# A planner's rule for split loads: a SyncE transfer no longer waits, in the virtual clock, for another part of its tile

## The chip, the cores and the metric
One core of one Trainium2 chip runs the program. The metric is the device time of one execution in microseconds (us). Three runs of the kernel before took 1041.17, 1041.32 and 1042.38 us; the median is 1041.32. A separate execution was profiled: it took 1042.86 us, and its span, from the first to the last instruction, is 1040.8 us.

## What is computed
Agent attention, then a mixture of experts in which each token goes to its best expert. B=4 batches, N=11456 tokens, C=128 channels, 49 agents, 8 experts, 1024 hidden columns, all float32.

```python
a2k = sm(agents, k)              # softmax of scaled products, 49 x N
agent_v = a2k @ v                # 49 x 128
q2a = sm(q, agents)              # N x 49
x = (q2a @ agent_v).reshape(B * N, 128)
e_idx = argmax(x @ w_gate)       # one expert for each token
for e in range(8):
    h = maximum(x[mask] @ w1[e], 0)
    out[mask] = gate_w * sigmoid(x @ w_output_gate)[e] * (h @ w2[e])
```

## The kernel before, in words
**Tiles and stages.** A batch is cut into 12 units, eleven of 1024 tokens and one of 192. For each unit of k the program makes scores `ks`, for each unit of v a share of the average `av`, and for each unit of q scores `qs`. The scores of q become weights `e16` (float16 pairs on 49+49+30 rows), which a transposing DMA turns into the tile `x1`. The last 19 rows of these pairs are then copied by four small DMAs, 19 partitions x 1024 columns of float16 (38 KB) each, into four places of a second tile `x2` (rows 32g to 32g+19, lines 1022 and 1023). A token's most frequent expert in the batch is picked first (`fold`, line 779): its weights `w1t`, `w2t` are loaded by an index read on SyncE (`ei`, line 834), folded with the average into `aw` and `w`, and the main stream runs all tokens through that expert. A tile of the main stream (512 tokens, 92 in all) has 16 matmuls `h` (for two halves, four from `x1`, four from `x2`) and 64 matmuls `y`. Between them ScalarE makes `hh` and VectorE makes `hl`, the high and low halves of the hidden layer. The few tokens of other experts are gathered and done again near the end (`let`, `lx`, `lh`, `ly`).

**What sets the order.** Every engine runs its own instructions in the order in which the program was written out, and that order comes from a planner. The planner keeps a virtual clock (`Clock`, from line 55): a time for each engine and one for the DMA engines together, and for each tile the time when it is written (`ready`) and read (`read`). Each piece of work is a coroutine that offers its next instruction; `can` (line 108) lets it through if the virtual clock says that its operands are there, and `issue` (line 120) or `emit` (line 195) books its cost. If nothing fits, TensorE's virtual time goes on by 40 ns, or, before the first tile of the main stream, a filler matmul `warm` is written out. So a wait in the virtual clock is no wait on the chip: it is other instructions, or fillers, put in front. On the chip an instruction waits for its own semaphores, whatever the plan thought.

**DMAs in the virtual clock.** A transfer from SyncE (SP) is booked in `emit`: it starts 1100 ns after SP issues it, or when the DMA engines are free, takes its bytes at 360 bytes per ns, and its tile is ready 950 ns later. For 19 x 1024 values this comes to 216 ns. The tile's `writer` is then "DMA":

```python
q = c.vt["DMA"] = max(c.vt["DMA"], t + 1100.0) + n * (2.46 if turned else 4.0) / 360.0
...
    c.ready[x.name] = max(c.ready.get(x.name, 0.0), q + (2500.0 if turned else 950.0))
    c.writer[x.name] = "DMA"
```

SP's own time goes on by 480 ns for each. In `at` (line 84) an instruction that writes a tile waits until the tile is ready, unless its own engine wrote it. For a second transfer into the same tile the engine is "SP" and the writer "DMA", so the rule holds it back until the transfer before has landed.

**Around the change.** Tiles that SP writes in parts: `x2` (four parts, 48 units), `w1t` (two halves, four batches), the first unit of k (two halves, line 592), and `wgo`. In `q_rest` (line 991) the order is: transposing DMA into `x1`, the four parts of `x2`, then the gate matmuls `lg` from `x1`; each `yield` must pass before the next is offered. The main stream takes a unit only when `x1` and `x2` are ready in the virtual clock (`can1` in `main_stream`, line 1245). Once the main stream has started, a matmul that reads a DMA's tile is held 1500 ns longer (`LANDS`, line 52); before that there is no margin. Loads go into 7 large places that become free when TensorE has read them, `x1` and `x2` into 8 small ones.

Of the kernel before, what the change touches and what calls it, by code (L numbers as in the profile page):

```python
# [15 lines left out]
SP = mybir.EngineType.SP  # L16
# [38 lines left out]
class Clock:  # L55
# [28 lines left out]
    def at(self, ins, outs=(), eng=None, late=None):  # L84

        t = 0.0
        for x in ins:
            if x.name not in self.apart:
                w = self.writer.get(x.name)
                if w == "DMA" and late is not None:  # L90
                    more = self.margin
                else:
                    more = 0.0 if w in (eng, "PE") else late or 0.0
                t = max(t, self.ready.get(x.name, 0.0) + more)
        for x in outs:
            n = x.name
            if n in self.apart:
                continue
            if self.writer.get(n) != eng:
                t = max(t, self.ready.get(n, 0.0))  # L100
            t = max(t, self.read.get(n, 0.0), self.free_at(n))
        return t
# [158 lines left out]
def agent_attention_top1_moe(ctx, tc, qT, kT, v, aT, wg, wo, w1, w2, cst, out):  # L261
# [144 lines left out]
    def agents_split():  # L406

        sq = wk.tile([P, B], F32, name="asq", tag="asq", bufs=1)
        for b in range(B):
            yield from ACT.q.activation(ah[:, b, :], at[:, b, :], AF.Square, accum_out=sq[:, b:b + 1])  # L410
        yield from wait_free()
        r = bank("as_r")
        mark = hold()
        yield from PE.q.matmul(r[:, 0:B], ones, sq, start=True, stop=True)
        s, si = yield from scale(r[:, 0:B], "as", 14, B)
        release(mark)
        bc = s.unsqueeze(2).broadcast_to([P, B, A2])
        a_ = wk.tile([P, 4, C], F32, name="a_s", tag="os", bufs=4).rearrange("p t c -> p (t c)")[:, 0:B * A2].rearrange("p (b a) -> p b a", a=A2)
        yield from DVE.q.tensor_tensor(a_, at, bc, op=ALU.mult)
        yield from ACT.q.copy(ah, a_)  # L420
        yield from DVE.q.tensor_tensor(al, a_, ah, op=ALU.subtract)
        yield from DVE.q.tensor_copy(asi, si)
# [183 lines left out]
    def scores(item, name):  # L606

        kind, b, u = item
        base, pp, nt = UNITS[u]
        whole = item in WHOLE  # L610
        while item not in (parts if whole else halves):
            yield None
        yield from wait_free(True)
        if whole:
            x, inv = parts.pop(item), None
            todo = [(x, at)]
        else:
            xh, xl, inv = halves.pop(item)
            todo = [(xh, ah), (xh, al), (xl, ah)]
        s = bank(name)  # L620
        mark = hold(True)
        for t in range(nt):
            if whole and pp == P and not clk.started:

                for h in range(0, P, 64):
                    yield from PE.q.matmul(s[h:h + 64, t * A2:(t + 1) * A2], x[:, t * pp + h:t * pp + h + 64],
                                           at[:, b, :], start=True, stop=True)
                continue
            for k, (x, a) in enumerate(todo):
                yield from PE.q.matmul(s[0:pp, t * A2:(t + 1) * A2], x[:, t * pp:(t + 1) * pp], a[:, b, :],  # L630
                                       start=(k == 0), stop=(k == len(todo) - 1))
        scored(item)
        if not whole:
            scored_n[0] += 1
        return s, mark, inv
# [1092 lines left out]
```

## Time and profile before

| what | value |
|---|---|
| median of three runs | 1041.32 us |
| the profiled execution | 1042.86 us, span 1040.8 us |
| TensorE (PE) busy | 1001.8 us, 96% |
| VectorE (DVE), ScalarE (ACT), GpSimd (POOL) busy | 817.4, 673.8, 431.7 us |
| mean granted TensorE clock | 0.988 |
| DMA packets of SyncE's queue | 142.86 MB, 51.3% of 16 engines' span |
| first `h` of the main stream | 69.68 us |
| first `y` | 75.86 us |
| parts of `x2` | 176 DMAs of 38.0 KB, 16 of 7.1 KB |

All times are counted from the start of the span. In a row of a timeline the columns are start, duration, engine, line, operation, output<-input, and a count where equal instructions are merged; brackets tell of idle time before it and what ended it. SPq is SyncE's queue: its durations are those of issuing, not of moving data. Every recorded instruction goes through one helper, so all have line 211 and are told apart by their tiles' names. Names in the profile have no numbers: `x_ld` is `x1` or `x2`, and `x_ld<-x_ld` is a part of `x2`. A float32 matmul stands there as two.

### The profile page before, as it was taken

The page shows a single profiled execution, that of the slowest core. Times are in us where ns is not written, and L with a number is a line of the kernel's source. Part 1 is how long each engine was busy: PE and PEld are TensorE (multiplying, and loading weights), DVE is VectorE, ACT ScalarE, POOL GpSimd, SP SyncE. Part 2 cuts the span into 40 slices and gives each one's busy share as a digit, 9 for nine tenths or more (in the row PEclk, how much of TensorE's full clock was granted, in tenths as well). Part 3 has the DMA queues.
Part 4 walks back from the last instruction along what each step waited for, and adds up shares of the span by engine and source line. Part 5 has one row for each costly group of instructions (what it writes and reads, how often), then busy time and mean ns, then how long its engine had stood idle before and what let it go on. Part 6 is the DMA issues. An engine that isn't in the chain of part 4 may idle for free. (4 is left out here: it accounts for less than half of the span.)

```text
span 1040.8 us, 28670 instructions
## 1 busy us (share of the span) xinstructions
PE 1001.8 (96%) x11098; PEld 794.4 (76%) x11098; DVE 817.4 (79%) x2167; ACT 673.8 (65%) x1523; POOL 431.7 (41%) x722
## 2 busy tenths in 40 slices
PE   9899989999999999999999999999999999999996
PEld 8668767777788777777687688787777688888765
DVE  2757668788888888698978888889999877755773
ACT  3355657786867877777778777657665565655542
POOL 1402446463343465563244565532333455443111
PEclk9999999999999999999999999999999999999998
DMA  8957835646267843755396444445342554644111
GB/s 297 300 136 231 169 96 135 154 137 162 71 165 196 159 127 90 149 156 146 101 198 158 136 125 144 123 123 171 82 106 58 135 137 160 148 138 159 37 34 68
DMA packets 106367, 146.20 MB, mean 140 GB/s; under 512 B 60466, under 2 KB 69094, under 8 KB 106228
## 3 DMA queue, kind: packets, MB, share of 16 engines
q1 hardware_dynamic: 104884, 142.86, 51.3%
q0 software_dynamic: 1344, 1.49, 0.7%
q8 instruction: 88, 1.44, 0.6%
q14 instruction: 51, 0.42, 0.1%
HBM read 90.88 MB, written 35.17 MB: 121 GB/s over the span
## 5 line engine op out<-in xcount | busy, mean ns | idle before, releaser
L211 PE MATMUL y<-vv,hh 128*128 128x256 f16 (+1 forms) x2880 | 592.8, 274 | 14.6 <-DVE xsq_s L211 3.5
L211 PE MATMUL y<-vv,hl 128*128 128x128 f16 (+1 forms) x2880 | 535.5, 220 | 0.7
L211 DVE SCALAR_TENSOR_TENSOR hl<-h,hh 128x512 f16<-128x512 f32 (+1 forms) x736 | 448.0, 667 | 83.4 <-ACT hh L211 82.0
L211 ACT ACTIVATE hh<-h 128x512 f16<-128x512 f32 (+1 forms) x736 | 372.9, 591 | 190.3 <-PE h L211 189.8
L211 PEld LDWEIGHTS <-hh 128*128 128x128 f16 (+1 forms) x2880 | 283.4, 98 | 63.4 <-issue 36.3
L211 PEld LDWEIGHTS <-hl 128*128 128x128 f16 (+1 forms) x2880 | 316.8, 110 | 16.5 <-issue 11.7
L211 PE MATMUL h<-x_ld,w 128*128 128x512 f16 (+1 forms) x1472 | 280.6, 379 | 5.0 <-DVE hl L211 3.6
L211 PEld LDWEIGHTS <-w 128*128 128x128 f16 x1472 | 93.0, 100 | 91.1 <-issue 69.7
L211 POOL TENSOR_TENSOR os<-os,smt 128x512 f32<-128x512 f32 (+1 forms) x92 | 96.7, 1051 | 126.5 <-DVE os L211 78.5
L211 DVE TENSOR_TENSOR os<-y,ys 128x256 f32<-128x256 f32 x180 | 74.6, 415 | 39.5 <-ACT ys L211 38.9
L211 ACT COPY ys<-y 128x256 f32<-128x256 f32 x180 | 68.4, 380 | 57.2 <-PE y L211 56.8
L211 PEld LDWEIGHTS ks<-at,k_ld 128*64 128x64 f32 (+2 forms) x960 | 90.3, 164 | 8.2 <-issue 4.6
L211 PE MATMUL ks<-at,k_ld 128*64 128x50 f32 (+2 forms) x960 | 94.7, 235 | 0.6 <-DVE os L211 0.5
L211 PE MATMUL av<-ev,v_ld 128*128 128x50 f32 x540 | 85.5, 245 | 0.0
L211 PEld LDWEIGHTS av<-ev,v_ld 128*128 128x128 f32 x540 | 82.1, 191 | 2.6 <-ACT hh L211 0.8
L211 POOL TENSOR_TENSOR ev<-S,km_o 128x400 f32<-128x400 f32 (+1 forms) x44 | 42.3, 965 | 61.6 <-PE av L211 46.8
L211 POOL TENSOR_TENSOR e<-ef,e 128x392 f16<-128x392 f32 (+1 forms) x48 | 42.0, 876 | 60.3 <-ACT e L211 59.9
L211 POOL TENSOR_TENSOR q_ld<-q_ld,xhq 128x1024 f16<-128x1024 f32 (+1 forms) x28 | 55.0, 1963 | 21.9 <-ACT q_ld L211 18.2
L211 PEld LDWEIGHTS qs<-at,q_ld 128*128 128x128 f32 (+2 forms) x340 | 46.2, 183 | 4.7 <-issue 2.2
L211 PE MATMUL qs<-at,q_ld 128*128 128x50 f32 (+2 forms) x340 | 47.6, 242 | 0.0
L211 PEld LDWEIGHTS <-xhq 128*128 128x128 f16 (+1 forms) x412 | 34.1, 97 | 12.6 <-issue 5.6
L211 PE MATMUL lh<-lxs,lw_ld 128*128 128x128 f32 x224 | 42.4, 276 | 0.5 <-ACT lxs L211 0.4
(273 smaller groups left out, 1357.7 us busy)
## 6 DMA issues: line engine op xcount, KB each, us to landing
q_ld<-qT SPq DMA_DIRECT2D x44, 512.0 KB
v_ld<-v SPq DMA_DIRECT2D x44, 512.0 KB
out<-os SPq DMA_DIRECT2D x88, 256.0 KB
k_ld<-kT SPq DMA_DIRECT2D x43, 512.0 KB
lw_ld<-w SPq DMA_DIRECT2D x28, 512.0 KB
efd<-ef SPq DMA_DIRECT2D x44, 200.0 KB
x_ld<-x_ld SPq DMA_DIRECT2D x176, 38.0 KB
w1t<-w SPq DMA_DIRECT2D x8, 256.0 KB
```

Of the source, the lines that this page charges most:

```text
L211: return getattr(self.eng, op)(*a, **k)
```

## The change
In `at`, which tells when an instruction may start, the rule for a tile that was already written has one more exception. If the tile's writer is a DMA and the instruction comes from SP, the time when the tile is ready no longer counts. What else holds a transfer stays: the readers of the tile, the buffer before it in the same place, and its inputs.

```diff
             n = x.name
             if n in self.apart:
                 continue
-            if self.writer.get(n) != eng:
+            w = self.writer.get(n)
+            if w != eng and (w, eng) != ("DMA", "SP"):
                 t = max(t, self.ready.get(n, 0.0))
             t = max(t, self.read.get(n, 0.0), self.free_at(n))
         return t
```

On the chip the parts of `x2` go to different partitions and wait for no other part, before or after. All instructions are the same in kind and number but for the fillers: 202 `warm` matmuls before, 159 after. What moves is the order on every engine.

The first place is SyncE's queue around the choice of the first batch's expert. `x10_1` and `x20_1` are `x1` and `x2` of batch 0, unit 1; `k1_3` is unit 3 of batch 1's k; `ei0` the index, `w1t0` and `w2t0` the weights. Before:

```order
L211 DMA x20_0_ld_779<-x10_0_ld_768 19x1024
L211 DMA k1_3_ld_910<-kT 128x1024
L834 TENSOR_LOAD ei0_1013
L211 ISA
L211 DMA w1t0_1031<-w1 128x512
L211 DMA x20_0_ld_779<-x10_0_ld_768 19x1024
L211 ISA
L211 DMA w1t0_1031<-w1 128x512
L211 ISA
L211 DMA w2t0_1104<-w2 128x1024
L211 DMA x20_0_ld_779<-x10_0_ld_768 19x1024 x2
L211 DMA_TRANSPOSE x10_1_ld_1163<-e16_1_91 128x8x128
```

After that come the store `avnd`, four parts of `x20_1`, and the loads of `k1_4`, `k1_5`, `q0_2` and `k1_6`. Now:

```order
L212 DMA x20_0_ld_743<-x10_0_ld_732 19x1024 x4
L212 DMA_TRANSPOSE x10_1_ld_868<-e16_1_91 128x8x128
L212 DMA k1_3_ld_880<-kT 128x1024
L835 TENSOR_LOAD ei0_981
L212 ISA
L212 DMA w1t0_1000<-w1 128x512
L212 ISA
L212 DMA w1t0_1000<-w1 128x512
L212 ISA
L212 DMA w2t0_1003<-w2 128x1024
L212 DMA x20_1_ld_874<-x10_1_ld_868 19x1024 x4
L212 DMA k1_4_ld_1131<-kT 128x1024
```

The four parts of unit 0 and the transposing DMA of unit 1 have moved ahead of the index, the three loads of weights follow one another, and four parts of unit 1 stand in a row right ahead of the load of `k1_4`. The loads of `k1_5`, `q0_2` and `k1_6` follow it. The same holds further on: the four parts of a unit stand in a row in the whole queue.

The second place is TensorE's order between the folded weights `aw` and the first matmul `h` of the main stream (`mw` is a sum over the weights, `avn` a transpose of the average). Before:

```order
L211 MATMUL mw0_r_1156<-sq0_1108,ones_86 128x1 x2
L211 MATMUL aw0_3_1167<-w1t0_1031,avd_0_94 128x512
L211 MATMUL avn0_1188<-kc_71,avd_0_94 49x128
L211 LDWEIGHTS idle_x_78
L211 MATMUL warm_1197<-idle_x_78 128x256
...
L211 LDWEIGHTS w0_1_1206
L211 MATMUL h0_0_0_1258<-x10_0_ld_768,w0_1_1206 128x512
```

What is left out is 19 more fillers. Now:

```order
L212 MATMUL aw0_3_1149<-w1t0_1000,avd_0_94 128x512
L212 MATMUL ks1_4_1141<-at_74,k1_4_ld_1131 64x50 x4
L212 MATMUL avn0_1165<-kc_71,avd_0_94 49x128
L212 MATMUL ks1_4_1141<-at_74,k1_4_ld_1131 64x50 x12
L212 LDWEIGHTS idle_x_78
L212 MATMUL warm_1195<-idle_x_78 128x256
L212 MATMUL ks1_5_1191<-at_74,k1_5_ld_1133 64x50 x16
...
L212 MATMUL qs0_2_1219<-at_74,q0_2_ld_1135 64x50 x16
...
L212 MATMUL ks1_6_1249<-at_74,k1_6_ld_1137 64x50 x4
L212 LDWEIGHTS w0_1_1187
```

Twenty fillers have become six beside the scores of `k1_4`, `k1_5`, `q0_2` and two tiles of `k1_6`, which before stood between the matmuls `y` of the main stream. (A score before the main stream is written as two matmuls of 64 rows, later as one of 128: 26 scores of 128 rows have moved ahead of the first `h`, and 15 more stand between the first `h` and the first `y`.) Further ahead, between the scores of batch 0's second unit of k and its `qs` of unit 0, 55 fillers have become 36; ahead of `qs` of unit 1 there is one more. Between the matmul `ga`, from which the index is made, and the first `h`, 48 fillers have become 24, the scores have grown from 3 units to 6.2, and eight `lg` of unit 1 have come in.

## The prediction
> **What bounds the kernel now.** I read the page's busy times first, then the windows of 26 us, then what TensorE waited for, then the timelines of TensorE and of SyncE's queue.
>
> ```profile
> span 1040.8 us, 28670 instructions
> ...
> PE 1001.8 (96%) x11098; PEld 794.4 (76%) x11098; DVE 817.4 (79%) x2167; ACT 673.8 (65%) x1523; POOL 431.7 (41%) x722
> ```
> ```profile
> 0.00:26.00 26.00, 24.93 (x445) 21.27 (x447) 6.38 (x18) 7.89 (x23) 3.12 (x17) 1.00 0.86 298
> ...
> 52.00:78.00 26.00, 24.19 (x258) 16.44 (x257) 15.30 (x48) 13.51 (x33) 1.84 (x7) 0.91 0.57 135
> ...
> 104.00:130.00 26.00, 24.85 (x271) 20.54 (x270) 17.97 (x42) 17.98 (x38) 11.21 (x16) 1.00 0.88 169
> 130.00:156.00 26.00, 21.63 (x224) 16.78 (x223) 18.18 (x47) 14.64 (x33) 10.85 (x17) 0.93 0.37 95
> ...
> 1014.00:1040.00 26.00, 16.79 (x152) 13.91 (x151) 8.65 (x30) 7.05 (x20) 4.85 (x6) 0.83 0.20 69
> ```
> ```profile
> PE y L211 <- DVE xsq_s L211: 3.1, 1, 3.1
> PE y L211 <- DVE os L211: 1.3, 1, 1.3
> PE y L211 <- DVE lL L211: 1.1, 1, 1.1
> ```
>
> TensorE is busy for 1001.8 of 1040.8 us, so an order can win time in three ways: fewer fillers, cheaper places for the scores, fewer stalls. Of the 39 us idle, 1.8 lie in 52 to 78, 5.5 in 104 to 156 (waits for VectorE, with the clock at 0.93 in the second window) and 9.2 in the last window, whose matmuls the change leaves in their order. The places to look at are the start and the first units of the main stream.
>
> **The start, up to the index.**
>
> ```profile
> 10.41 1.38 PE L211 MATMUL warm<-idle_x 128*128 128x256 f16 x11
> ...
> 11.78 1.58 PE L211 MATMUL warm<-idle_x 128*128 128x256 f16 x13
> 13.29 1.14 PE L211 MATMUL ks<-at,k_ld 128*64 128x50 f32 x32
> ...
> 54.91 0.29 PE L211 MATMUL ga<-wgs,ones 128*128 128x8 f32 x2
> ...
> 62.68 1.88 PE L211 MATMUL aw<-w1t,avd 128*128 128x512 f32 x4
> ...
> 67.88 1.97 PE L211 MATMUL warm<-idle_x 128*128 128x256 f16 x16 [0.24 <-ACT avn_sb L211]
> 69.68 0.81 PE L211 MATMUL h<-x_ld,w 128*128 128x512 f16 x3
> ...
> 75.86 0.38 PE L211 MATMUL y<-vv,hh 128*128 128x256 f16 x1
> ```
>
> From 11.78 to 13.29, 13 fillers take 1.51 us, 0.116 each. Eighteen fewer ahead of `qs` of unit 1 are **2.1 us**. No score here waits for a DMA. The third one would stand at 11.2 instead of 13.29; some 1.8 MB (`at`, `kc` and three units of k: 98 + 155.5 + 3 x 512 KB) must have come by then, which at the first window's 298 GB/s take 6.2 us. I take the whole 2.1 and move `ga` from 54.91 to 52.8. Were the loads later than this, it would be 1.0 or less.
>
> **From the index to the first `h`.**
>
> ```profile
> 44.57 0.77 SPq L211 DMA_DIRECT2D x_ld<-x_ld  x1
> ...
> 56.78 0.35 SPq L211 DMA_DIRECT2D w1t<-w  x1
> 57.18 0.67 SPq L211 DMA_DIRECT2D x_ld<-x_ld  x1
> 58.06 0.35 SPq L211 DMA_DIRECT2D w1t<-w  x1
> 58.64 0.33 SPq L211 DMA_DIRECT2D w2t<-w  x1
> ...
> 68.30 2.47 SPq L211 DMA_DIRECT2D x_ld<-x_ld  x4
> 70.87 0.85 SPq L211 DMA_DIRECT2D k_ld<-kT  x2
> ```
> ```profile
> 133.93 1.85 SPq L211 DMA_DIRECT2D x_ld<-x_ld  x3
> ```
> ```profile
> 135.00:136.00 1.00, 1.00 (x16) 0.81 (x13) 0.00 (x0) 0.78 (x3) 1.00 (x1) 0.89 0.07 12
> ...
> 138.00:139.00 1.00, 0.05 (x1) 0.05 (x1) 1.00 (x3) 0.08 (x1) 0.00 (x0) 1.00 0.06 25
> 139.00:140.00 1.00, 1.00 (x9) 0.83 (x9) 1.00 (x2) 0.00 (x0) 0.97 (x1) 1.00 0.07 27
> ...
> 141.00:142.00 1.00, 1.00 (x14) 1.00 (x14) 0.57 (x2) 1.00 (x3) 0.15 (x1) 1.00 0.00 0
> ```
> ```profile
> 46.00:48.00 2.00, 0.60 (x5) 0.17 (x2) 1.65 (x5) 0.60 (x2) 0.00 (x0) 1.00 1.07 420
> ```
>
> The three parts of `x2` issued at 133.93 are alone in flight. The DMA share is then 0.06 to 0.07, one engine of 16, at 25 to 27 GB/s. So a part of 38 KB holds one engine for about 1.5 us, four hold it for 6.1, and data flow some 2 us after issue. A load of 512 KB runs at 420 GB/s over all engines, 1.25 us. The plan books 0.2 us for a part. Before, its rule that each part waits for the last spaced them by 1100 + 216 + 950 = 2266 ns, longer than 1.5; now they go 480 ns apart, and the plan thinks them landed far too early.
>
> [...]
>
> By rows: the first half of `w1t` is issued at 56.78 - 2.1 = 54.7. Without the part between them (57.18), the three weights go out by 55.5; 1 MB at 420 GB/s, 2 us after issue, is in at 59.2. The four parts of unit 1 stand behind, to 65.3, then `k1_4` at 66.5, `k1_5` 67.8, `q0_2` 69.0, `k1_6` 70.3. TensorE's way from `ga` to the first `h` was 14.77; 24 fillers less (-2.8), 3.2 units of scores more (1.07 net each, +3.4) and eight `lg` (+0.3) make 15.7, so 68.5 without a wait. Since it meets the loads in order, `qs` ends at 70.1, five fillers and two tiles more make **71.0**. That is 1.3 later than 69.68, in spite of the 2.1 won. If nothing queues on one engine it is -1.2; if unit 0's parts and the transposing DMA ahead of the index hold up the weights too, 2.5 later than I say, +3.8. I take +1.3, on which the rows of 133 to 142 bear directly.
>
> **What the main stream no longer carries.**
>
> ```profile
> 78.01 0.27 PE L211 MATMUL y<-vv,hh 128*128 128x256 f16 x1
> ...
> 78.17 0.27 PE L211 MATMUL y<-vv,hh 128*128 128x256 f16 x1
> ```
> ```profile
> 80.12 0.28 PE L211 MATMUL y<-vv,hh 128*128 128x256 f16 x1
> 80.24 0.32 PE L211 MATMUL ks<-at,k_ld 128*128 128x50 f32 x2
> ...
> 80.45 0.27 PE L211 MATMUL y<-vv,hh 128*128 128x256 f16 x1
> ```
>
> A pair of `y` takes 0.16 us, with a score between 0.33: a score costs 0.165. The 26 that go ahead of the first `h` save **4.3 us**. The 15 between first `h` and first `y` (69.68 to 75.86 before) take 2.5 us; about 1.5 of it fits into the 1.8 idle of 52 to 78, so **1.5 us**. VectorE and ScalarE get the work of unit 2 there earlier; I count that at nothing, since TensorE's wait for the loads covers it, and up to 1 us if it doesn't.
>
> **Further on.**
>
> ```profile
> 437.09 2.10 SPq L211 DMA_TRANSPOSE x_ld<-e  x1
> ...
> 443.29 1.85 SPq L211 DMA_DIRECT2D x_ld<-x_ld  x3
> ```
> ```profile
> 448.40 0.21 PE L211 MATMUL lg<-gs,x_ld 128*128 128x36 f16 x2
> ```
>
> `lg` stands behind the four parts in its coroutine. Here `x1` was in by 443.29, when the parts that read it were issued, and `lg` came 5.1 us later, the tightest of the 48 units. Now the plan offers `lg` 3 x (2266 - 480) = 5.4 us sooner, so the tightest come to about zero, on an engine that works in order. I allow +1.0 in all, between 0 and 9. Where the clock falls to 0.5 in a stall I count nothing, since 52 to 78 has such a stretch already (0.91).
>
> [...]
>
> **Sum:** +1.3 - 4.3 - 1.5 + 1.0 = **-3.5 us**. Against the profiled execution's 1042.86 that is 1039.4 (span 1037.3); it lies 1.5 above the median, so against the median of 1041.32 it is **1037.8**.
>
> **Rivals.** *More is won:* the parts no longer make the plan believe units 2 to 4 late, the main stream keeps more finished `h` ahead, and the stalls of 104 to 156 go too, 5.5 idle and 1.8 for the clock (0.07 of 26). That gives -10.8, 1030.5. For it speaks that these waits are for VectorE just behind; against it that every new order has stalls of its own. *Nothing is won:* the parts of unit 0 and the transposing DMA, both now ahead of the index, hold up the weights and the loads behind them; the first `h` comes at 74.5, and the sum is zero, 1041.3. *Slower:* `lg` of units 2, 3 and 4 meets a transposing DMA that stands behind another unit's four parts, 6.1 us of one engine, and waits 3 us each time. Then 9 in place of 1.0, +4.5, 1045.8; it decides from 6.6 us of such waits. For it speaks that the plan is now further from the chip; against it, that none of TensorE's waits of 104 to 156 is for a DMA. That the change does nothing is ruled out by the order.
>
> **How the numbers follow.** The forecast has 0.42, more won 0.18, nothing won 0.18, slower 0.22. Some 0.2% (2 us) is what a measurement of this kernel can tell from no change; so faster 0.60, same 0.18, slower 0.22. The forecast's own range is 1035.3 (loads unhindered, -6.0) to 1039.2. The range of 8 in 10 reaches from 1031.5, short of the whole of the first rival, to 1045.8.
>
> **What would show it.** Right: `ga` near 52.8; a wait of TensorE of 2 to 4 us before the first `h`, at a score whose load was issued behind four parts; first `h` near 71; the whole main stream after it some 3 to 5 us sooner. Wrong: first `h` before 69 or after 74; a `y` or `lg` of units 2 to 4 waiting over 6 us in all; or a stretch after 180 that gains or loses over 3 us by itself.

## The result, and the profile after

The change makes the kernel slower: 1053.39 us (median of four runs, 1052.39 to 1054.63) against 1041.53 (median of four runs of the kernel before), a ratio of 1.0114 (95% interval 1.0096 to 1.0131). All ratios below are to runs of the kernel before on the same chip; a ratio leaves disturbed runs out, so it can differ by 0.1% from the quotient of two medians.

The page of the changed kernel, its first lines:

```profile
span 1052.8 us, 28695 instructions
...
PE 1002.5 (95%) x11109; PEld 791.6 (75%) x11109; DVE 826.1 (78%) x2167; ACT 671.3 (64%) x1523; POOL 428.2 (41%) x722
```

TensorE is idle for 50.3 us instead of 39.0. Its busy time has hardly moved (1001.8 to 1002.5), though 43 fillers of 0.116 us are gone, in part because more of it runs at a lower clock: (1 - 0.985) x 1052.8 = 15.8 us lost to the clock against (1 - 0.988) x 1040.8 = 12.5.

The windows at the places that the prediction named (columns: window, length, busy time and count of PE, PEld, DVE, ACT, POOL, granted clock, DMA share, GB/s):

```profile
0.00:26.00 26.00, 24.93 (x483) 21.37 (x485) 7.55 (x20) 8.69 (x25) 3.11 (x17) 1.00 0.91 330
52.00:78.00 26.00, 21.24 (x280) 15.69 (x277) 12.20 (x40) 10.21 (x25) 1.34 (x5) 0.93 0.77 262
104.00:130.00 26.00, 24.72 (x270) 19.25 (x270) 21.43 (x60) 18.82 (x44) 14.43 (x24) 1.00 0.65 100
130.00:156.00 26.00, 25.11 (x275) 19.87 (x274) 24.23 (x60) 18.35 (x42) 14.58 (x26) 1.00 0.50 132
```

In 52 to 78 the idle time has grown from 1.8 to 4.8 us, the price of the start; in 104 to 156 it has fallen from 5.5 to 2.2. So far the change gains: unit 9 of batch 0 begins at 254.0 instead of 259.5. Then it loses. Counting the 5760 matmuls `y` in both traces, numbers 1400 to 4000 take 15.2 us longer (428.8 against 413.6), 4500 to 5000 another 7.1, and the last 760 give back 10.5. These last two belong together in part: 14 `lh` and 16 `ly` of the left-over tokens have moved from the last stretch into the one named before. Of the 15.2, TensorE's idle time makes 7.2 (16.3 against 9.1) and the clock 5.1 (none was lost there before).

What TensorE now waits for (columns: total us, times, longest):

```profile
PE xrq L212 <- ACT xhq L212: 7.0, 6, 1.8
PE ks L212 <- DMA k_ld<-kT: 4.4, 2, 3.7
PE y L212 <- DVE c L212: 3.5, 2, 1.8
```

None of these three stood in the list of before with over 0.3 us. The second is the wait of the start that was forecast. The first is new: `xrq` is a sum over the squares `xhq`, which ScalarE makes from a unit of q as soon as its load has landed. ScalarE's waits for that load, in before and in after:

```profile
ACT xhq L211 <- DMA q_ld<-qT: 0.8, 2, 0.5
```
```profile
ACT xhq L212 <- DMA q_ld<-qT: 14.0, 8, 3.0
```

One of these eight, link by link, in the timelines of SyncE's queue, of ScalarE and of TensorE after the change:

```profile
316.74 2.45 SPq L212 DMA_DIRECT2D x_ld<-x_ld  x4
319.23 0.43 SPq L212 DMA_DIRECT2D q_ld<-qT  x1
```
```profile
323.99 0.54 ACT L212 COPY S<-ks 128x400 f32<-128x400 f32 x1
327.25 1.06 ACT L212 ACTIVATE xhq<-q_ld 128x1024 f16<-128x1024 f32 x1 [2.73 <-DMA q_ld<-qT]
```
```profile
326.29 0.32 PE L212 MATMUL ks<-at,k_ld 128*128 128x50 f32 x2
328.46 0.16 PE L212 MATMUL xrq<-xqq,ones 128*128 128x1 bf16 x1 [1.84 <-ACT xhq L212]
```
```profile
328.00:333.00 5.00, 4.54 (x36) 4.27 (x36) 4.08 (x8) 3.11 (x8) 1.04 (x1) 0.66 0.24 48
```

The load of q stands right behind the four parts of a unit's `x2` and takes 8.0 us to land. The semaphore events in the trace show where the time goes: fifteen of its sixteen completions are in by 322.88, the last comes at 327.23, behind that of the fourth part (326.00). The DMA share between the two is 0.06 to 0.09 (windows of about 1 us from 322.9 to 327.2): one engine of sixteen was late, and the load with it. It is so with all eight: each load stands behind four parts, with at most one other transfer between, and its last completion comes 2.0 to 4.4 us after the fifteenth. ScalarE, done at 324.5, waits 2.73 us for it; TensorE, which works in order, meets `xrq` and waits 1.84; and the five microseconds behind that are granted a clock of 0.66. In before the parts of this stretch were issued in ones and twos, with loads and stores between them:

```profile
318.27 1.24 SPq L211 DMA_DIRECT2D x_ld<-x_ld  x2
...
323.80 0.60 SPq L211 DMA_DIRECT2D x_ld<-x_ld  x1
326.78 0.33 SPq L211 DMA_DIRECT2D q_ld<-qT  x1
327.17 0.60 SPq L211 DMA_DIRECT2D x_ld<-x_ld  x1
```

The start, TensorE's timeline and SyncE's queue after:

```profile
51.33 0.39 PE L212 MATMUL ga<-wgs,ones 128*128 128x8 f32 x2
...
67.98 0.44 PE L212 MATMUL ks<-at,k_ld 128*64 128x50 f32 x8 [3.69 <-DMA k_ld<-kT]
...
74.45 1.36 PE L212 MATMUL h<-x_ld,w 128*128 128x512 f16 x8
...
80.78 0.28 PE L212 MATMUL y<-vv,hh 128*128 128x256 f16 x1
```
```profile
42.29 2.60 SPq L212 DMA_DIRECT2D x_ld<-x_ld  x4
45.01 5.43 SPq L212 DMA_TRANSPOSE x_ld<-e  x1
...
56.31 2.52 SPq L212 DMA_DIRECT2D x_ld<-x_ld  x4
58.94 1.20 SPq L212 DMA_DIRECT2D k_ld<-kT  x2
```
```profile
49.00:50.00 1.00, 1.00 (x16) 0.80 (x16) 0.13 (x2) 0.26 (x1) 0.00 (x0) 1.00 0.07 27
50.00:51.00 1.00, 1.00 (x28) 0.81 (x25) 0.56 (x3) 0.14 (x1) 0.25 (x1) 1.00 0.06 25
```

While the first four parts are alone in flight the DMA share is 0.06 to 0.07: one engine of 16. Their completions, by the semaphore events in the trace, lie at 49.18, 50.72, 52.25 and 53.86, 1.5 us apart; those of the second four, among loads, at 60.71, 62.81, 64.80 and 66.73, 2.0 apart, and `k1_4`, issued behind them, lands at 67.85. TensorE's `ks` begins 0.13 later.

### The profile page after: what moved, and what is told of

Same layout as the page of the kernel before. It is cut to its first block, busy times and chain, and to the rows that moved or that the text cites. A ratio compares the mean times of both kernels' runs of the same rounds, so it can differ in the third digit from the quotient of the medians.

```text
span 1052.8 us, 28695 instructions
## 1 busy us (share of the span) xinstructions
PE 1002.5 (95%) x11109; PEld 791.6 (75%) x11109; DVE 826.1 (78%) x2167; ACT 671.3 (64%) x1523; POOL 428.2 (41%) x722
## 5 line engine op out<-in xcount | busy, mean ns | idle before, releaser
L212 PEld LDWEIGHTS <-hl 128*128 128x128 f16 (+1 forms) x2880 | 312.8, 109 | 18.5 <-issue 13.6
L212 POOL TENSOR_TENSOR e<-ef,e 128x392 f16<-128x392 f32 (+1 forms) x48 | 42.2, 879 | 51.0 <-ACT e L212 50.3
```

The costliest lines, as they stand in the source:

```text
L212: return getattr(self.eng, op)(*a, **k)
```

## The experiments

Theory A: the time is lost because four parts in a row hold up loads on one DMA engine, at every unit and not only at the start. Theory B: the new order is worse by itself, wherever its transfers land.

**The orders unchanged, the parts spread.** A part is given more partitions than are read, and the planner books it as before, so every engine's order stays what it was to the instruction.

```diff
-            yield from SY.q.dma_start(x2[32 * g:32 * g + AR, 0:nt * pp], x1[AD:A, 0:nt * pp])
+            yield from SY.q.dma_start(x2[32 * g:32 * g + 32, 0:nt * pp], x1[AD:AD + 32, 0:nt * pp])
...
             n = min(_free(x) * x.shape[0] for x in outs + [y for y in ins if len(y.shape) > 1])
+            if outs[0].name.startswith("x2"):
+                n = n * AR // 32
```

On the changed kernel (e1_after_wide):

> The changed order to the instruction, but each part of x2 copies 32 partitions instead of 19 (the 13 extra rows are never read; the planner books the part as before). If a part then uses all 16 DMA engines, no load stands behind one busy engine. Theory A (the time is lost because loads of q land late behind four one-engine parts: ScalarE's waits of xhq for q_ld are 14.0 us after, 0.8 before): these waits fall under 3 us, TensorE's waits of xrq for xhq (7.0 us) under 1.5, the wait of 3.7 us before the first h goes too, and the time comes to 1035 to 1041 us. Theory B (the new order is itself worse at the changes of batch, wherever its transfers land): the waits of ScalarE go, but the time stays at 1047 us or more. If a part of 32 rows still holds one engine, the run is as after or slower, and says nothing of A.

Measured: 1037.47 us, ratio 0.9954 (0.9932 to 0.9975). ScalarE's waits, the same load of q as above in SyncE's queue, its reader, and the start:

```profile
ACT xhq L214 <- DMA q_ld<-qT: 0.8, 1, 0.8
```
```profile
310.46 3.19 SPq L214 DMA_DIRECT2D x_ld<-x_ld  x4
313.86 0.42 SPq L214 DMA_DIRECT2D q_ld<-qT  x1
```
```profile
319.28 1.11 ACT L214 ACTIVATE xhq<-q_ld 128x1024 f16<-128x1024 f32 x1
```
```profile
54.08 0.39 PE L214 MATMUL ga<-wgs,ones 128*128 128x8 f32 x2
...
70.83 1.36 PE L214 MATMUL h<-x_ld,w 128*128 128x512 f16 x8
```

The load again stands behind four parts, ScalarE again wants it some 5.4 us after its issue, and now nobody waits. In after thirteen loads of q stand right behind four parts; they took 4.0 to 9.1 us to land, 7.8 in the median. The same thirteen took 3.5 to 5.3 in e1, 3.9 in the median. `xrq` no longer waits for `xhq` at all. The four parts of unit 0 land 0.2 to 0.3 us apart (50.92, 51.24, 51.46, 51.68). Since the order is the same, the two traces can be laid side by side, counting `y`:

| stretch | after, us | e1, us | difference |
|---|---|---|---|
| start to `ga` | 51.33 | 54.08 | +2.75 |
| `ga` to first `y` | 29.45 | 24.64 | -4.81 |
| `y` 1 to 1000 | 162.11 | 161.01 | -1.10 |
| `y` 1000 to 1500 | 85.65 | 81.71 | -3.94 |
| `y` 1500 to 2000 | 82.64 | 81.19 | -1.45 |
| `y` 2500 to 3000 | 92.59 | 88.66 | -3.93 |
| `y` 4500 to 5000 | 107.56 | 105.32 | -2.24 |
| all others | | | 0.0 |

From the first `y` on the differences come to 12.7 us. Some 10.5 of it sit at waits for loads of q behind parts and at the slow clock right behind them: at 103, 128, 315 to 334 and 553 to 573 us of after (granted clock 0.92 from 318 to 340 and 0.89 from 560 to 575, against 1.00 in both windows of e1). Another 3.7 do not: at 261 and 844 both executions have the same wait of TensorE (1.77 and 0.67 us), but only after is granted half clock behind the first (0.50 from 261 to 264; windows 259 to 265 of after and 256 to 262 of e1: 0.72 and 1.00); behind the second after has 0.50 from 845 to 851, in `y` 4500 to 5000, the stretch that is 2.2 us longer; and 0.7 lies at 910. Against that e1 has a slow stretch of its own at the first `y` (0.57 from 75 to 83), which costs it 1.6. (Of the first 2.8, 1.1 are the first loads of the program, which came later in this execution, and the rest is slow clock from 48 to 51.5, 0.50 to 0.53 in the windows of 1 us from 48 to 51, where after has 1.00.) Theory B as the whole is out.

On the kernel before (e2_before_wide), the same edit as a control:

> The order of before to the instruction, with parts of 32 partitions as in the run with the changed order. Theory A: before has only 0.8 us of waits of xhq for q_ld, so little is to be won: 1038 to 1042 us. Theory B: the same. It is the control: what 32 rows are worth by themselves, without the change.

Measured: 1041.14 us, 0.9999 (0.9972 to 1.0025). Spread parts are worth nothing to the order of before that this measurement can tell (some 2.7 us either way); the price is not the parts', but that of four in a row.

One row more instead of 13 (e9_after_20_rows), the order again that of after:

```diff
-            yield from SY.q.dma_start(x2[32 * g:32 * g + AR, 0:nt * pp], x1[AD:A, 0:nt * pp])
+            yield from SY.q.dma_start(x2[32 * g:32 * g + 20, 0:nt * pp], x1[AD:AD + 20, 0:nt * pp])
...
+            if outs[0].name.startswith("x2"):
+                n = n * AR // 20
```

> The changed order to the instruction; each part of x2 copies 20 partitions, one more than needed (the 20th row is never read). [...] Rival: what helped with 32 rows was something else than the number of engines (the rows' alignment, say); then 20 rows stay at 1050 us or more.

Measured: 1036.86 us, 0.9960 (0.9945 to 0.9975); parts land 0.19 us apart (48.10, 48.29, 48.47, 48.66). That is as with 32 rows, and the rival's 1050 is out.

```profile
ACT xhq L214 <- DMA q_ld<-qT: 1.3, 1, 1.3
```

So one more row does what 13 do, by the medians; the trace of e9 is of its slowest run, with slow clock at the start (0.50 from 47 to 49), and its first `h` says nothing here. The semaphore events show how far a part is spread: one completion comes late in after, ten in e9 and sixteen in e1, and the parts land 1.53, 0.19 and 0.2 to 0.3 us apart. That a late completion stands for an engine in use is read from this and from the DMA share of 0.06 to 0.07 while the parts of after were alone in flight. Why 20 rows are spread over more of them than 19 is not shown: the runs have 19, 20 and 32 rows and no other count.

**Parts of the change.** Without its effect on `x2` (e3_after_x2_waits):

```diff
-            if w != eng and (w, eng) != ("DMA", "SP"):
+            if w != eng and ((w, eng) != ("DMA", "SP") or n.startswith("x2")):
```

> The change without its effect on x2: only w1t, the first unit of k and wgo go out without waiting; a part of x2 waits for the part before, as in the kernel before. Theory A: the four parts are 2.3 us apart again in the plan, so waits of xhq for q_ld are 0 to 3 us and the time is 1037 to 1044 us. Theory B (any new order can meet such stalls at the changes of batch): the time may lie anywhere from 1036 to 1053, and over 1047 would speak for B.

Measured: 1044.62 us, 1.0044 (1.0019 to 1.0068), with 1.4 us of waits of `xhq` for q: 0.6 above A's range. The large loss comes with the parts of `x2`, but this order is a little slower than before without it.

The rule only until the main stream starts (e4_start_only), only afterwards (e6_late_only):

```diff
-            if w != eng and (w, eng) != ("DMA", "SP"):
+            if w != eng and ((w, eng) != ("DMA", "SP") or self.started):
```
```diff
-            if w != eng and (w, eng) != ("DMA", "SP"):
+            if w != eng and ((w, eng) != ("DMA", "SP") or not self.started):
```

> The changed rule only until the main stream starts; from then on each part waits as before. Theory A: the wait of 3.7 us before the first h stays and the start is the same as after; the waits of xhq for q_ld after 140 us go, and what the start won (unit 5 of batch 0 came 4.9 us sooner) is kept: 1035 to 1039 us. Theory B: the time depends on how the order falls at the changes of batch, 1036 to 1053.

> The mirror image: until the main stream starts each part waits as before, afterwards the changed rule, with narrow parts. Theory A: the first h comes as in before (69 to 71), nothing is won there, and the four parts in a row hold up loads of q from 90 us on: waits of xhq for q_ld of 8 us or more, 1046 to 1056 us. Theory B: no such link; the time may be anywhere from 1036 to 1053 with few such waits.

Measured: 1036.16 us for the start only, 0.9956 (0.9943 to 0.9969), and 1060.45 for the rest only, 1.0168 (1.0135 to 1.0201), above A's 1056. In the first the wait of the start is there and the late waits are not (1.7 us of `xhq` for q); in the second `xhq` waits 12.0 us, and `lg` once waits for a transposing DMA that was issued behind four parts, as the prediction's slower rival had it:

```profile
ACT xhq L212 <- DMA q_ld<-qT: 12.0, 7, 2.8
```
```profile
PE lg L212 <- DMA x_ld<-e: 1.5, 1, 1.5
```

TensorE at the start of e4:

```profile
67.39 0.67 PE L212 MATMUL ks<-at,k_ld 128*64 128x50 f32 x8 [4.20 <-DMA k_ld<-kT]
...
74.36 1.36 PE L212 MATMUL h<-x_ld,w 128*128 128x512 f16 x8
```

The same two with parts of 32 partitions, the orders unchanged (e5_start_only_wide, e10_late_only_wide; the edits are those above, together):

> The changed rule until the main stream starts and parts of 32 partitions in the whole kernel, planned as if they had 19. With narrow parts this order took 1036.2 us and still had the wait of 4.2 us of TensorE for a load of k behind four parts, with a stretch of half clock behind it. Theory A (one DMA engine per part): the wait and the half clock go, some 5 to 6 us, and the first h comes 16 to 17 us behind ga instead of 23; 1030 to 1033 us, which beats both kernels. Theory B (the order decides, not the landing): 1036 as with narrow parts.

> The order of the run with the changed rule only after the main stream has started (1060.5 us with narrow parts), to the instruction, with parts of 32 partitions. Theory A: the 12.0 us of waits of xhq for q_ld and what they cost on TensorE go, 11 to 14 us: 1046 to 1050 us. What is then left above the kernel before (1041) is the order itself, 5 to 9 us, as between the wide runs with the rule everywhere (1037.5) and at the start only (1032.0). Theory B alone (order, not landing): 1057 or more.

Measured: 1032.00 us, 0.9906 (0.9876 to 0.9935), and 1045.06, 1.0039 (1.0018 to 1.0061). TensorE at the start of e5:

```profile
51.21 0.39 PE L214 MATMUL ga<-wgs,ones 128*128 128x8 f32 x2
...
67.96 1.36 PE L214 MATMUL h<-x_ld,w 128*128 128x512 f16 x8
```

From `ga` to the first `h` it is 16.75 us, in e1 too (70.83 - 54.08), against 23.24 in e4 (51.12 to 74.36) and 23.12 in after. So the parts cost the start 6.4 us up to the first `h`; up to the first `y`, around which the four traces have slow clock in different places (0.83 from 66 to 76 in after, 0.57 from 75 to 83 in e1; in e4 from 78.96 and in e5 from 73.04 an `h` takes 0.63 us, against 0.38 at 81.10 in e5), it is 4.8 (after against e1) and 6.7 (e4 against e5). In the order of e6 they cost 15.4 us by medians, 13.4 by ratios; e5 came out as A expected, e10 1 us below its range, and neither is near B's.

**The plan told the cost** (e7_booked), and its order with spread parts (e11_booked_wide):

```diff
+            if outs[0].name.startswith("x2"):
+                n = 1500.0 * 360.0 / 4.0
```

> The changed rule everywhere and narrow parts, but the planner books for each part 1500 ns of the DMA engines, about what the chip showed (landings 1.53 us apart), instead of 216. The plan then knows that a load behind four parts comes late, and writes other work in front. Theory A: waits of xhq for q_ld fall to 0 to 3 us and the time comes to 1035 to 1044 us. Theory B: 1036 to 1053, whatever these waits are.

> The order of the run that books 1500 ns for a part (1049.4 us), to the instruction, with parts of 32 partitions. There a load of q that was issued at 99.38, ahead of four parts, landed with them at 111.14, and ScalarE waited 8.9 us for it. Theory A, enlarged (a part on one engine also holds up a load issued shortly ahead of it): this one wait goes, with TensorE's 6.4 us behind it and a stretch of half clock, 7 to 10 us: 1039 to 1043 us. If the load was late for another reason: 1047 or more.

Measured: 1049.36 us, 1.0057 (1.0027 to 1.0088), and 1044.09, 1.0024 (1.0003 to 1.0046): both above what A expected. In e7 one wait is left, and it is the longest of all. SyncE's queue, ScalarE and TensorE there:

```profile
99.38 0.33 SPq L214 DMA_DIRECT2D q_ld<-qT  x1
99.80 2.70 SPq L214 DMA_DIRECT2D x_ld<-x_ld  x4
102.62 5.12 SPq L214 DMA_TRANSPOSE x_ld<-e  x1
```
```profile
111.16 1.06 ACT L214 ACTIVATE xhq<-q_ld 128x1024 f16<-128x1024 f32 x1 [8.89 <-DMA q_ld<-qT]
```
```profile
113.08 0.37 PE L214 MATMUL y<-vv,hh 128*128 128x256 f16 x1 [6.41 <-DVE os L214]
```

The load stands ahead of the parts, not behind them, and lands with the last of them: eleven of its sixteen completions are in by 105.05, the last five come from 111.09 to 111.14. The parts alone do not do this. In after 24 other loads were issued right ahead of four parts, and all landed 3.4 to 5.2 us after their issue, before the parts did. What is special here is the transposing DMA right behind the parts, issued while the load was still in flight. The other loads so placed are those of k at 41.91 in after, 41.70 in e4 and 41.64 in e7, and they took 11.1 to 12.0 us. With spread parts ScalarE's wait is 3.2 instead of 8.9 us, and TensorE's longest wait of `y` for `os` 1.4 instead of 6.4. Booking the time of the parts helps the loads behind them and not this one ahead. The enlarged theory holds in that narrow parts are needed for the wait, and its price was 5.3 us by medians (3.4 by ratios), not 7 to 10; as a rule for any load just ahead of four parts it is refuted by the 24. That it takes the transposing DMA is read from these cases; no run took it away.

**A small change of another kind** (e8_before_lands_1600), and its order with spread parts (e12_lands_1600_wide):

```diff
-LANDS = 1500.0
+LANDS = 1600.0
```

> A control of how far any small change of the plan moves the time: the kernel before with LANDS at 1600 ns instead of 1500. By theory A such changes are worth a few us either way, 1037 to 1046; theory B needs that a reshuffled order can lose 12 us, so a time over 1049 would speak for it.

> The order of the kernel before with LANDS at 1600 ns (1052.6 us), to the instruction, with parts of 32 partitions. Its waits of xhq for q_ld are 4.3 us, three of them, against 14.0 after the change. Theory A alone: those go and no more, 1047 to 1050 us, and the rest of the 11 us lost is in the order (waits of y for VectorE and ScalarE at 279, 284, 348, 367, 534, 809). If it comes to 1043 or less, narrow parts were the whole of that loss too; if it stays over 1050, the order alone was.

Measured: 1052.55 us, 1.0088 (1.0071 to 1.0105), and 1055.40, 1.0121 (1.0098 to 1.0145). That is what theory B needed. The waits of TensorE in e12:

```profile
PE y L213 <- DVE xsq_s L213: 5.2, 3, 3.1
PE y L213 <- DVE os L213: 4.5, 4, 1.4
PE y L213 <- DVE hl L213: 3.6, 3, 2.1
```

Here late transfers are a small part (2.5 us of waits of `xhq` for q, and 2.2 of `let` for a DMA near the end); the order itself puts `y` in front of what VectorE has not yet done. A reshuffle can thus cost as much as the change did, by another way. With spread parts the changed rule everywhere was still 5.5 us above the rule at the start only (1037.47 against 1032.00). To see whether that is the rule's or a reshuffle's, four runs with spread parts and another LANDS:

> The changed rule everywhere, parts of 32 partitions, LANDS at 1600 ns instead of 1500. If the 5.5 us left belong to the changed rule in the main stream: 1035 to 1040 us, near the 1037.5 of 1500. If any reshuffle moves the time by some 10 us, as LANDS 1600 did to the kernel before: anywhere from 1032 to 1053.

> The changed rule everywhere, parts of 32 partitions, LANDS at 1550 ns. The rule's own cost: 1035 to 1040 us. Reshuffle: anywhere from 1032 to 1053, and not tied to the time at 1600.

> The rule of before, parts of 32 partitions, LANDS at 1550 ns. The rule decides: 1039 to 1044 us, and the 1055 at 1600 is one bad place. Reshuffle: anywhere from 1036 to 1056.

> The changed rule until the main stream starts, parts of 32 partitions, LANDS at 1600 ns (it acts only after the start, so the start is the same as in the run of 1032.0 us). The rule decides: 1030 to 1035 us. Reshuffle: anywhere from 1031 to 1046, and if the rule of before loses 14 us by LANDS 1600 itself, the same here, 1043 to 1046.

Two lie in the range of the rule (e13, e16), two below it (e14 by 6 us, e15 by 2). e14 lies below the 1032 of the reshuffle too: nothing that was expected allowed for so fast an order. Medians and ratios of all orders by rule, side by side:

| rule, parts | LANDS 1500 | 1550 | 1600 |
|---|---|---|---|
| before, 19 rows | 1 | | 1052.55, 1.0088 |
| before, 32 rows | 1041.14, 0.9999 | 1036.96, 0.9966 (0.9955 to 0.9978) | 1055.40, 1.0121 |
| start only, 19 rows | 1036.16, 0.9956 | | |
| start only, 32 rows | 1032.00, 0.9906 | | 1034.45, 0.9926 (0.9902 to 0.9949) |
| everywhere, 19 rows | 1053.39, 1.0114 | | |
| everywhere, 32 rows | 1037.47, 0.9954 | 1029.10, 0.9894 (0.9878 to 0.9911) | 1036.04, 0.9937 (0.9912 to 0.9961) |

Under one rule, 50 ns of a margin move the time by 8.4 us (changed) and up to 18 us (before). The 5.5 us lie within that, so they are not shown to be the rule's; what makes one of these orders better than another stays open. The fastest kernel of all is the changed rule with spread parts and LANDS at 1550, e14, better than both kernels; its first lines and one of its waits:

```profile
span 1027.1 us, 28680 instructions
...
PE 992.0 (97%) x11109; PEld 785.8 (77%) x11109; DVE 817.8 (80%) x2167; ACT 670.5 (65%) x1523; POOL 427.8 (42%) x722
```
```profile
PE y L214 <- DVE c L214: 3.5, 2, 1.8
```

The waits of `y` for `c`, which after has and before does not, stand in the fastest kernel too; they don't tell a slow order from a fast one.

## Why the prediction was wrong

Forecast 1037.8, measured 1053.39: outside the range, and on the other side.

- **The bound** was right: TensorE is busy for 96% of the span in before, 95% in after and e8 and 97% in e14, and the time is decided by what its order waits for.
- **The start as a whole** came out right, in part by luck. The terms +1.3, -4.3 and -1.5 make -4.5; the rule at the start only gives 1036.16, a ratio of 0.9956, which is -4.6 us. But the terms were not right one by one. The first `h` came 4.8 us later than before, not 1.3, and from there to number 640 of `y` (187.0 against 192.3) after won 10.0 us, where the scores were counted at 5.8. The surplus of 4.2 is no more than what the first rival named: the idle time of 104 to 156 fell by 3.3, and its clock rose from 0.93 to 1.00 in the second window, worth 1.8. The scatter between orders (below) is larger than any of this.
- **Fillers ahead of the index**, -2.1: `ga` was forecast at 52.8 and came at 51.33 (e4: 51.12, e5: 51.21). In before, TensorE's wait of 2.1 us for `den` ahead of it is followed by slow clock (0.72 from 48 to 54, worth 1.7 us); in after a wait of the same length is not (1.00 from 46 to 52), and that is about the 1.5 by which it came sooner than forecast. In e1, whose order up to there is the same, it is (0.72 from 47 to 53), and `ga` came at 54.08. So the count of fillers was right, and the rest is the clock.
- **From the index to the first `h`**: the mechanism was right, a wait of 3.69 us at a score behind four parts, the size was off. That a load waits for the parts ahead of it was the author's estimate: in before no load follows the three parts of 133.93 until 142.96. After shows it: `k1_4` landed at 67.85, the fourth part ahead of it at 66.73. Without the wait the way was put at 15.7 us and is 16.75; the parts were priced at 2.5 us and cost 6.4. They land 2.0 us apart among other loads, not 1.5, and the wait is followed by slow clock: the window from 66 to 76 has a granted clock of 0.83 in after and 0.97 in e1 (whose own slow stretch begins at 75.4, behind its first `h`). The first `h` came at 74.45, the rival's 74.5, and only in part by the rival's way: the weights did land 8.6 us after `ga` (59.95), where the forecast had 6.4, but TensorE waited for `k1_4` and not for them. With spread parts the changed start is worth 9 us (e5 against e2).
- **"Further on", +1.0 in all: this step failed.** It measured +17.2 us (1053.39 - 1036.16). The text asked only who reads `x1`, and priced a delay of `lg`; `lg` waited for no unit's transfer in after. It had shown, with the rows of 133 to 142, that a part holds one engine for 1.5 us, and used that for loads that TensorE reads itself before the first `h`, and for `lg` in a rival. The same four parts stand in a row in front of loads at every unit, and it did not follow those loads to their first reader. That is ScalarE, which wants a unit of q some 5.3 us after its issue (319.23 to 324.5), and a load takes 7.8 in the median behind four parts. Some 10 to 15 us of the 17.2 are shown to be this, by orders that were held fixed (after against e1, from the first `y` on: 12.7, of which 10.5 at the loads themselves; e6 against e10: 15.4 by medians, 13.4 by ratios). The rest is within what a reshuffle does and is not settled.
- **The argument against the slower rival**, that no wait of TensorE in 104 to 156 was for a transfer, was read from the trace of before, in which the planner spaced the parts and put other transfers between them. That spacing is what the change takes away. And TensorE's list would not have shown it: there the wait carries ScalarE's name.
- **Rivals.** The sign of the slower rival was right and its mechanism wrong: the wait of `lg` that it named stands in no place of after, and once, with 1.5 us, in e6. The stalls of the first rival did shrink, as said above. What was named as a warning, a stretch after 180 that loses over 3 us by itself, is what happened, at 259 to 372 and at 470 to 620.

## What to carry to other kernels

When a change puts several transfers in a row, list every transfer that is then issued behind them in the same queue (and just ahead, where a transposing DMA follows), and follow each to its first reader on any engine: here the wait of ScalarE for a load stood in TensorE's list under ScalarE's name. Count the engines that a small copy uses: one padding row, 20 for 19, cost 5% more bytes here and took away a loss of 16 us (1053.39 to 1036.86). And in a kernel whose order comes out of a planner, two orders are compared only after the order itself has been held fixed, or after the scatter of orders has been measured: 50 ns of a margin moved this one by more than most of the terms.

## What was unexpected of the hardware

- A load was held up by transfers behind it. The load of q of e7, issued 0.4 us ahead of four parts and a transposing DMA, landed at 111.14 and the last part at 111.13; in after a load of k issued at 41.91, in the same place, landed at 53.89 and the last part at 53.86, while the load of k before it took 6.3 us. There fifteen of its sixteen completions came between 53.72 and 53.89, while each part has one late completion: engines were late that, by this reading, no part was on. The 24 loads ahead of four parts with no transposing DMA behind them were not held (3.4 to 5.2 us). Why was not tried.
- A transposing DMA issued right behind four parts of 19 rows held SyncE's queue for 5.43 us in after (5.12 in e7); in e1, behind four parts of 32 rows at the same place, 1.29. The next load in after was issued at 50.55, right behind it.
- A wait of 1.84 us was followed by slow clock (0.66 over 5 us); at the same matmuls in e1, without the wait, the window from 321 to 326 has 1.00. But a wait of 1.77 us at one and the same matmul was followed by slow clock in after (0.72 from 259 to 265) and not in e1 (1.00 from 256 to 262), and the wait of 2.1 to 2.2 us for `den` was followed by it in before and in e1 (0.72 in both) and not in after (1.00). What decides it is not shown.
- Executions of one order scatter: e1's ten runs reach from 1029.64 to 1040.88 us. Part of that may be the clock behind equal waits, which differed between traces at `den` and at 261; it was not followed further.
